# Seven block products in place of eight for the last matmul of an attention and feed-forward kernel

## The chip, the cores and the metric

The kernel runs on one core of a Trainium2 chip. The time is that of the device for one execution, in microseconds (us). Before the change it is 239.63 us, the median of three runs (239.34 to 240.02).

## The reference, cut to what matters

```python
q_s = softmax(q, axis=-1)                       # q, k, v: 8 batches, 8 heads, 576 tokens, 64 wide
k_s = softmax(k, axis=tokens)
kv = einsum('bhsd,bhse->bhde', k_s, v)
x = einsum('bhsd,bhde->bhse', q_s, kv)          # laid out as 4608 tokens x 512
a, b = x @ w1, x @ w2                           # 4608 x 1024 each
out = ((a * b) @ w3) @ w_out                    # 4608 x 512
```

## The kernel before

Both last weights are folded once: `W3O = w3 @ w_out` (1024 x 512) is made by `fold`, so that the feed-forward part is `(a * b) @ W3O`. Inputs are float32; the operands of TensorE are float16.

The work has two halves. `attention(b)`, for the batches 0 to 7, makes the 512 main tokens of its batch (`x`, as float16) and the 64 that remain of it (`xtail`). `chunk(c)`, for c = 0 to 7, takes the main tokens of batch c, and chunk 8 all the tails. The steps of a batch are: row maximum of q (`qmx`, L582), subtraction (`qsub`, L587), exponential on ScalarE (`qexp`, L595), sum (`qsm`, L600), a small number added (`qeps`, L606 or L608), reciprocal (`qrc`, L612), product (`qn`, L619) and a transpose by DMA (`qd`), each in two parts; for k a maximum (`kmx`, L489 or L498 to L501, then `cba`, `cbx`, `cb`), a subtraction (`ksub`, L524) and an exponential (`kexp`, L532); v is cast (`vc`). `kv` (L549) multiplies k and v, `kve` and `kv2` (L566 to L575) scale the result, `xm` and `xt` (L667) apply it to the transposed q, and `xs`, `xts` copy the products to `x` and `xtail`.

A chunk has eight pairs of `up` steps (L784), of four matmuls each with 512 moving columns (in the chunks 0 and 1, which are cut in two halves of tokens, eight with 256). The pair's first product goes to SBUF by `bs`, on ScalarE or VectorE; VectorE then multiplies it with the second, which it reads from PSUM (`ab`, L799). Four `down` steps follow, one for each 128 tokens (L806, for chunk 8 L821): eight matmuls with 512 moving columns over `ab` and `W3O`. `os` copies their bank to SBUF, and `st` stores it with two DMAs.

A list of 795 names, `ORDER`, sets what stands before what on each engine, and `PICKS` which engine takes a step that could run on several. Each engine works through its own part of the list in order and waits at each step for what that needs. Rings of buffers add waits: four PSUM banks for `up` (`pab`), two for `down` (`po`), two for attention, two `ab` tiles; so `ab` of chunk c overwrites that of chunk c - 2. Steps marked as `port` have two inputs in SBUF, or are GpSimd's (`qsub`, `ksub`, `qn`, the `kmx` of batches 0 to 3, some casts). Where two of them that follow each other in the list are on different engines, `run` makes the second wait for the first. It does so for the list's first 580 entries (`LINKED`), up to about `xm` of batch 6.

Of the kernel before, what the change touches and what calls it, by code (L numbers as in the profile page):

```python
# [101 lines left out]
up.1.2.0.3 up.0.2.0.3 down.1.2 kexp.3.1 kv.3 qmx.4.1 bs.2.0.3 os.1.1 qn.3.1 qd.3.1 qn.3.0 vc.4.1
qsub.4.1 qmx.4.0 ab.2.0.2 kmx.4.0 kve.3 up.1.2.0.4 up.0.2.0.4 os.1.2 kv2.3 bs.2.0.4 up.1.2.0.5 xt.2
bs.2.0.5 xts.2.1 qexp.4.1 down.1.3 ab.2.0.3 up.0.2.0.5 xts.2.0 ab.2.0.4 os.1.3 qd.3.0 xm.3.0 xm.3.1
xt.3 qmx.5.0 cba.4 ab.2.0.5 xs.3.0.0 cbx.4 xts.3.1 up.1.2.0.6 up.0.2.0.6 xts.3.0 xs.3.1.0 xs.3.0.1
cb.4 qsub.4.0 qsub.5.0 vc.4.0 xs.3.1.1 bs.2.0.6 st.1.0 qsm.4.1 ab.2.0.6 up.1.2.0.7 up.0.2.0.7
up.1.3.0.0 up.0.3.0.0 bs.2.0.7 qeps.4.1 qrc.4.1 ab.2.0.7 down.2.0 st.1.2 up.1.3.0.1 up.0.3.0.1 k.5
down.2.1 qexp.4.0 qsm.4.0 qeps.4.0 qexp.5.0 ksub.4.1 bs.3.0.0 kexp.4.1 ksub.4.0 kexp.4.0 qrc.4.0
st.1.1 v.5 qn.4.0 bs.3.0.1 os.2.0 st.1.3 qd.4.0 up.1.3.0.2 kv.4 kve.4 os.2.1 down.2.2 qn.4.1 kmx.5.1
kmx.5.0 cba.5 qmx.5.1 kv2.4 down.2.3 cbx.5 bs.3.0.2 qd.4.1 ab.3.0.0 up.0.3.0.2 ab.3.0.1 xm.4.0  # L110
os.2.2 os.2.3 xm.4.1 cb.5 ab.3.0.2 xt.4 xts.4.0 xs.4.0.0 up.1.3.0.3 xts.4.1 up.0.3.0.3 qsm.5.0
up.1.3.0.4 xs.4.1.0 qsub.5.1 qexp.5.1 bs.3.0.3 qeps.5.0 up.0.3.0.4 up.1.3.0.5 ab.3.0.3 q.6 bs.3.0.4
st.2.0 k.6 ksub.5.0 xs.4.1.1 ab.3.0.4 up.0.3.0.5 up.1.3.0.6 bs.3.0.5 qsm.5.1 qrc.5.0 up.0.3.0.6
ab.3.0.5 up.1.3.0.7 up.0.3.0.7 ksub.5.1 qn.5.0 xs.4.0.1 kexp.5.0 vc.5.0 bs.3.0.6 qeps.5.1 kexp.5.1
vc.5.1 ab.3.0.6 up.1.4.0.0 up.0.4.0.0 qrc.5.1 bs.3.0.7 qmx.6.1 ab.3.0.7 kv.5 down.3.0 down.3.1
st.2.1 qd.5.0 st.2.2 bs.4.0.0 kmx.6.0 kmx.6.1 os.3.0 up.1.4.0.1 down.3.2 os.3.1 qmx.6.0 kve.5 kv2.5
ab.4.0.0 qn.5.1 qd.5.1 up.0.4.0.1 xm.5.0 qsub.6.1 bs.4.0.1 qexp.6.1 os.3.2 xm.5.1 xt.5 xs.5.1.0
cba.6 ab.4.0.1 up.1.4.0.2 up.0.4.0.2 xts.5.0 xts.5.1 up.1.4.0.3 up.0.4.0.3 qsub.6.0 bs.4.0.2 qsm.6.1
ab.4.0.2 qexp.6.0 cbx.6 bs.4.0.3 xs.5.1.1 xs.5.0.1 qeps.6.1 cb.6 xs.5.0.0 ksub.6.0 v.7 q.7 ab.4.0.3
qrc.6.1 up.1.4.0.4 bs.4.0.4 up.0.4.0.4 up.1.4.0.5 bs.4.0.5 ab.4.0.4 up.0.4.0.5 ab.4.0.5 up.1.4.0.6  # L120
bs.4.0.6 qmx.7.0 up.0.4.0.6 up.1.4.0.7 up.0.4.0.7 ab.4.0.6 up.1.5.0.0 up.0.5.0.0 bs.4.0.7 down.3.3
up.1.5.0.1 qsm.6.0 st.3.1 ksub.6.1 kexp.6.1 kexp.6.0 qn.6.1 ab.4.0.7 st.3.0 v.6 vc.6.1 vc.6.0 kv.6
k.7 st.2.3 os.3.3 down.4.0 down.4.1 st.3.2 st.3.3 qd.6.1 qeps.6.0 bs.5.0.1 kve.6 os.4.0 os.4.1
kmx.7.0 kmx.7.1 qrc.6.0 qn.6.0 bs.5.0.0 ab.5.0.0 up.0.5.0.1 up.1.5.0.2 up.0.5.0.2 up.1.5.0.3
ab.5.0.1 kv2.6 qmx.7.1 bs.5.0.2 ab.5.0.2 qd.6.0 down.4.2 up.0.5.0.3 xm.6.0 bs.5.0.3 ab.5.0.3 cba.7
os.4.2 xm.6.1 xt.6 xts.6.0 xts.6.1 up.1.5.0.4 up.0.5.0.4 bs.5.0.4 up.1.5.0.5 ab.5.0.4 bs.5.0.5
xs.6.1.1 up.0.5.0.5 up.1.5.0.6 up.0.5.0.6 xs.6.0.1 cbx.7 xs.6.1.0 bs.5.0.6 ab.5.0.5 up.1.5.0.7
up.0.5.0.7 vc.7.0 xs.6.0.0 down.4.3 qsub.7.1 qsub.7.0 qexp.7.0 qexp.7.1 cb.7 ab.5.0.6 st.4.2 st.4.0
ksub.7.1 qsm.7.0 qeps.7.0 qrc.7.0 bs.5.0.7 ab.5.0.7 ksub.7.0 vc.7.1 up.1.6.0.0 up.0.6.0.0 up.1.6.0.1
up.0.6.0.1 st.4.1 qsm.7.1 kexp.7.1 bs.6.0.0 up.1.6.0.2 ab.6.0.0 up.0.6.0.2 kexp.7.0 kv.7 bs.6.0.1  # L130
qeps.7.1 ab.6.0.1 up.1.6.0.3 bs.6.0.2 up.0.6.0.3 up.1.6.0.4 qrc.7.1 ab.6.0.2 bs.6.0.3 ab.6.0.3
up.0.6.0.4 up.1.6.0.5 up.0.6.0.5 kve.7 bs.6.0.4 os.4.3 qn.7.1 qd.7.1 qn.7.0 qd.7.0 kv2.7 down.5.0
os.5.0 ab.6.0.4 down.5.1 os.5.1 bs.6.0.5 ab.6.0.5 down.5.2 up.1.6.0.6 os.5.2 bs.6.0.6 xm.7.0 xm.7.1
xt.7 xts.7.0 up.0.6.0.6 up.1.6.0.7 xs.7.0.1 xs.7.1.0 xs.7.0.0 xs.7.1.1 xts.7.1 up.0.6.0.7 up.1.7.0.0
bs.6.0.7 ab.6.0.6 up.0.7.0.0 up.1.7.0.1 bs.7.0.0 down.5.3 st.4.3 os.5.3 st.5.3 st.5.1 st.5.2
ab.6.0.7 ab.7.0.0 up.0.7.0.1 up.1.7.0.2 up.0.7.0.2 bs.7.0.1 up.1.7.0.3 ab.7.0.1 up.0.7.0.3 bs.7.0.2
up.1.7.0.4 ab.7.0.2 up.0.7.0.4 bs.7.0.3 up.1.7.0.5 ab.7.0.3 bs.7.0.4 ab.7.0.4 up.0.7.0.5 up.1.7.0.6
up.0.7.0.6 bs.7.0.5 ab.7.0.5 bs.7.0.6 up.1.7.0.7 ab.7.0.6 bs.7.0.7 up.0.7.0.7 ab.7.0.7 up.1.8.0.0
up.0.8.0.0 up.1.8.0.1 up.0.8.0.1 down.6.0 bs.8.0.0 bs.8.0.1 st.5.0 os.6.0 st.6.0 down.6.1 os.6.1
down.6.2 down.6.3 os.6.2 os.6.3 down.7.0 up.1.8.0.2 bs.8.0.2 down.7.1 st.6.1 st.6.2 ab.8.0.0  # L140
ab.8.0.1 st.6.3 os.7.0 os.7.1 down.7.2 up.0.8.0.2 up.1.8.0.3 ab.8.0.2 bs.8.0.3 up.0.8.0.3 up.1.8.0.4
up.0.8.0.4 ab.8.0.3 bs.8.0.4 ab.8.0.4 up.1.8.0.5 bs.8.0.5 up.0.8.0.5 up.1.8.0.6 bs.8.0.6 ab.8.0.5
up.0.8.0.6 ab.8.0.6 up.1.8.0.7 up.0.8.0.7 bs.8.0.7 ab.8.0.7 down.7.3 st.7.0 os.7.2 down.8.0 st.7.1
# [784 lines left out]
```

## Time and profile before

| What | Number |
|---|---|
| Median of three runs | 239.63 us |
| Span of the profiled execution, first to last instruction | 237.4 us |
| What the runs' median holds beside that span | 2.2 us |
| TensorE's granted clock, whole span | 1.00 |
| Busy in the span: TensorE | 230.1 us (97%) |
| VectorE | 180.3 us (76%) |
| ScalarE | 121.7 us (51%) |
| GpSimd | 110.0 us (46%) |

An execution's own time outside the profiler is not listed beside its span, so that the 2.2 us stand for what lies around it. The profile names engines PE (TensorE), PEld (its loading of weights), DVE (VectorE), ACT (ScalarE), POOL (GpSimd) and SP (the queue that issues DMAs). In a row of grouped instructions come the line, the engine, the operation, output and inputs with their shapes, the count, the busy time, the mean duration of one, and the idle time ahead of them. Consecutive instructions of one engine overlap a little, so the distance from start to start is shorter than a duration. Row by row in time, a row gives its start, its length (of several instructions where x2 or more stands at the end) and in brackets how long the engine was idle before it and what released it.

### The profile page before, as it was taken

Reading aid. Unit: us, or ns where it says so; the run is one execution under the profiler, and the core shown is the slowest. Engines: PE = TensorE matmul, PEld = TensorE weight load, DVE = VectorE, ACT = ScalarE, POOL = GpSimd, SP = SyncE. Lnnn points to the kernel's source line nnn. Section 1 sums busy time; section 2 is a strip of 40 time slices with the busy share of each in tenths; the row PEclk is TensorE's granted clock in tenths of the full one; section 3 lists DMA queues with packets and bytes.
Section 4 is the critical chain, followed back from the end, with each engine's and each line's share of the span. In section 5 each row is a group of like instructions: output and inputs, shape, how many; then the busy total and the mean of one; then the engine's idle time right before and its main releaser. Section 6 shows DMA issues by size and latency. Waiting matters only on the chain.

```text
span 237.4 us, 4860 instructions
## 1 busy us (share of the span) xinstructions
PE 230.1 (97%) x1935; PEld 119.5 (50%) x1935; DVE 180.3 (76%) x277; ACT 121.7 (51%) x221; POOL 110.0 (46%) x73
## 2 busy tenths in 40 slices
...
DMA packets 38742, 46.51 MB, mean 196 GB/s; under 512 B 17088, under 2 KB 22976, under 8 KB 38720
## 3 DMA queue, kind: packets, MB, share of 16 engines
...
q14 instruction: 7, 0.06, 0.1%
...
## 4 chain that ended last, share of the span: by engine, by line
PE 81%; DMA 8%; DVE 5%; POOL 4%; issue 1%; ACT 0%; POOLq 0%; ACTq 0%
PE pab L784 46%; PE po L806 22%; DMA w<-in_moe_w_dram 6%; PE po L457 4%; PE po L821 3%; PE pkv L549 2%; DMA qT<-en 2%; PE xm L667 1%; DVE qm L582 1%; POOL k L524 1%; PE w3t L445 1%; POOL en L619 1%; POOL w L406 1%; DVE ab L799 1%; DVE kmx L498 1%
## 5 line engine op out<-in xcount | busy, mean ns | idle before, releaser
L784 PE MATMUL pab<-x,w1sb 128*128 128x512 f16 (+1 forms) x320 | 65.9, 337 | 0.4 <-DVE kmx L499 0.4
L784 PE MATMUL pab<-x,w2sb 128*128 128x512 f16 (+1 forms) x320 | 66.0, 337 | 0.0
L799 DVE TENSOR_TENSOR ab<-pab,bsb 128x512 f16<-128x512 f32 x72 | 48.6, 682 | 20.2 <-PE pab L784 13.6
L806 PE MATMUL po<-W3O,ab 128*128 128x512 f16 x256 | 58.9, 379 | 0.0
L784 PEld LDWEIGHTS <-w1sb 128*128 128x128 f16 x352 | 34.2, 98 | 28.5 <-DMA w1sb<-in_moe_w_dram 0.6
L784 PEld LDWEIGHTS <-w2sb 128*128 128x128 f16 x352 | 33.5, 98 | 27.5 <-issue 0.7
L325 ACT CAST bsb<-pab 128x512 f16<-128x512 f32 x46 | 26.8, 582 | 35.8 <-PE pab L784 34.6
L524 POOL TENSOR_TENSOR k<-k,cb 128x1152 f32<-128x1152 f32 x12 | 31.4, 2628 | 16.4 <-issue 5.1
L806 PEld LDWEIGHTS <-ab 128*128 128x128 f16 x256 | 24.5, 98 | 28.5 <-issue 0.4
L587 POOL TENSOR_TENSOR q<-q,qm 128x1024 f32<-128x1024 f32 (+1 forms) x14 | 29.5, 2125 | 13.1 <-DVE rc L573 5.4
L325 ACT COPY osb<-po 128x512 f32<-128x512 f32 (+1 forms) x25 | 14.3, 571 | 40.3 <-PE po L806 26.8
L619 POOL TENSOR_TENSOR en<-eq,qr 128x1024 f16<-128x1024 f16 (+1 forms) x13 | 27.2, 2106 | 10.5 <-DVE qr L612 10.4
L582 DVE TENSOR_REDUCE qm<-q 128x20 f32<-128x1280 f32 (+1 forms) x16 | 21.2, 1340 | 3.6 <-DMA q<-in_q_dram 3.6
L325 DVE CAST bsb<-pab 128x512 f16<-128x512 f32 x26 | 17.6, 677 | 6.8 <-PE pab L784 6.3
L600 DVE TENSOR_REDUCE qr<-eq 128x20 f32<-128x1280 f16 (+1 forms) x16 | 21.5, 1341 | 1.5 <-ACT eq L595 1.4
L595 ACT ACTIVATE eq<-q 128x1280 f16<-128x1280 f32 (+1 forms) x16 | 18.5, 1161 | 4.8 <-DVE q L587 3.9
L532 ACT ACTIVATE ek<-k 128x1152 f16<-128x1152 f32 x16 | 18.2, 1163 | 3.8 <-POOL k L524 3.8
L489 DVE TENSOR_REDUCE km<-k 128x128 f32<-128x1152 f32 x8 | 16.9, 2149 | 0.0
L457 PE MATMUL po<-wosb,w3T 128*128 128x512 f16 x64 | 15.3, 379 | 0.5 <-DMA wosb<-in_moe_w_out_dram 0.5
L325 DVE COPY osb<-po 128x512 f32<-128x512 f32 x12 | 8.3, 688 | 9.1 <-PE po L806 7.9
L329 ACT ACTIVATE x<-xm 128x512 f16<-128x512 f32 x18 | 10.3, 597 | 6.4 <-PE xm L667 6.2
L325 ACT CAST v<-v 128x1152 f16<-128x1152 f32 x9 | 10.3, 1148 | 0.3 <-DMA v<-in_v_dram 0.3
...
## 6 DMA issues: line engine op xcount, KB each, us to landing
...
k<-in_k_dram SPq DMA_DIRECT2D x4, 1152.0 KB, 10.1
...
```

Source lines behind the costliest of these rows:

```text
L325: return [(nc.scalar.copy if eng == "ACT" else engine[eng].tensor_copy)(out=out, in_=in_)]
L457: nc.tensor.matmul(st["pf", ft], lhsT=st["w3T", ft][:, gt, :], rhs=wosb[:, gt, :], start=(gt == 0), stop=(gt == N_FT - 1))
L524: return [engine[eng].tensor_tensor(out=kb[:, two(hp), :, :], in0=kb[:, two(hp), :, :], in1=st["cb", b][:, two(hp), None, :].broadcast_to( ...
L532: nc.scalar.activation(out=st["ek", b][:, hp, :, :].rearrange("p j (i d) -> p i j d", i=2), in_=kb[:, two(hp), :, :], func=AF.Exp)
L582: dve.tensor_reduce(out=st["qm", b][:, :, j], in_=qb[:, :, j, :], axis=AX.X, op=ALU.max)
L587: return [engine[eng].tensor_tensor(out=qb[:, :, j, :], in0=qb[:, :, j, :], in1=st["qm", b][:, :, j, None].broadcast_to([P, HH, n, D]), op ...
L595: nc.scalar.activation(out=st["eq", b, p], in_=qb[:, :, j, :], func=AF.Exp)
L600: dve.tensor_reduce(out=st["qr", b][:, :, slice(*PARTS[p])], in_=st["eq", b, p], axis=AX.X, op=ALU.add)
L619: return [engine[eng].tensor_tensor(out=st["en", b][:, j, :, :].rearrange("p j h d -> p h j d"), in0=st["eq", b, p], in1=st["qr", b][:, :, ...
L784: nc.tensor.matmul(st["p", one, c, sub, u][:, a * (t1 - t0):(a + 1) * (t1 - t0)], lhsT=w[:, ct, fb * P:(fb + 1) * P], rhs=x()[:, ct, t0:t1 ...
L799: dve.tensor_tensor(out=st["ab", c][:, nf * u:nf * u + nf, t0:t1], in0=cut(st["p", 0, c, sub, u]), in1=cut(st["bsb", c, sub, u]), op=ALU.mult)
L806: nc.tensor.matmul(st["po", c, tb], lhsT=st["ab", c][:, ft, tb * P:(tb + 1) * P], rhs=W3O[:, ft, :], start=(ft == 0), stop=(ft == N_FT - 1))
```

## The change

For the chunks 2 to 7 (`SEVEN`), the four `down` steps become seven products of blocks. `ab` is cut into 2 x 2 blocks of 512 features by 256 tokens, `W3O` into 2 x 2 blocks of 512 features by 256 columns. Each product (`sp`) is two times four matmuls with 256 moving columns. The blocks that they need are sums:

- `sT.1` to `sT.4`, once for the whole kernel: four sums of blocks of `W3O`, 128 x 1024 in float16, two on VectorE and two on GpSimd. They are written to the tile of w3, which nothing reads after the fold.
- `sa.c.1` to `sa.c.4` for each chunk: four sums of blocks of `ab`, of the same size and type; 12 of the 24 on VectorE and 12 on GpSimd.

The results are put together in three PSUM banks, taken in turn from the ring of two. The products 1, 6, 5 and 3 add up in one; after each of the first three a copy of the bank's state goes to SBUF as float32 (`kept`, 128 x 512, 15 on ScalarE and 3 on VectorE), and the next product waits for that copy. Product 2 has a bank of its own, and 7 and then 4 share the third, where 4 waits until `os.c.22` has read it. Four blocks come out: 12 by a copy, and 11, 22 and 21 by VectorE, which adds a bank and a kept copy. Each is stored by two DMAs as before, with runs of 256 columns in place of 512.

`ab` of chunk c + 2 now waits for products and sums of chunk c. The ring of the kept copies (`w3T`) has three buffers instead of two. `LINKED` goes from 580 to 10000, so the chaining of `port` steps, the new sums among them, holds for the whole list. From the entry after `up.0.1.1.2` on (the 260th) the list is new, with 859 names, and so are the engines picked for it: `bs` has 53 steps on ScalarE where it had 46, `ksub` 13 on GpSimd where it had 12.

VectorE's queue, at the place where batch 4's row sums have been inverted and chunk 3 begins (L612 before, L622 after). Before (`ab_1318` is chunk 2's):

```order
L600 TENSOR_REDUCE qr_1596<-eq_1513 128x4x5
L799 TENSOR_TENSOR ab_1318<-pab_1576,bsb_1592 128x512
L612 RECIPROCAL qr_1596<-qr_1596 128x4x5
L799 TENSOR_TENSOR ab_1318<-pab_1604,bsb_1619 128x512
L600 TENSOR_REDUCE qr_1596<-eq_1655 128x4x4
L524 TENSOR_TENSOR k32_0_75<-k32_0_75,cb_1586 128x1152
L612 RECIPROCAL qr_1596<-qr_1596 128x4x4
```

Of the change (`ab_1328` is chunk 2's, `ab_1650` chunk 3's; `w316_90` is the tile that holds the sums):

```order
L622 RECIPROCAL qr_1548<-qr_1548 128x4x4
L622 RECIPROCAL qr_1548<-qr_1548 128x4x5
L811 TENSOR_TENSOR ab_1328<-pab_1599,bsb_1612 128x512
L592 TENSOR_REDUCE qm_1641<-q32_1_78 128x4x4
L811 TENSOR_TENSOR ab_1650<-pab_1620,bsb_1618 128x512
L592 TENSOR_REDUCE qm_1641<-q32_1_78 128x4x5
L811 TENSOR_TENSOR ab_1650<-pab_1636,bsb_1648 128x512
L983 TENSOR_TENSOR w316_90<-W3O_89,w316_90 128x1024
L854 TENSOR_TENSOR w316_90<-ab_1328 128x1024
L811 TENSOR_TENSOR ab_1650<-pab_1655,bsb_1745 128x512
L499 TENSOR_REDUCE km_1758<-k32_1_76 128x128
```

The `ksub` of batch 4 has left VectorE, and two sums stand between two `ab` steps; the first of them waits, by the chain, for GpSimd's `qn` of batch 4.

GpSimd's queue, from `qn` of batch 4 to `ksub` of batch 5. Before:

```order
L619 TENSOR_TENSOR en_1672<-eq_1655,qr_1596 128x4x4x64
L619 TENSOR_TENSOR en_1672<-eq_1513,qr_1596 128x4x5x64
L587 TENSOR_TENSOR q32_1_78<-q32_1_78,qm_1557 128x4x320
L524 TENSOR_TENSOR k32_1_76<-k32_1_76,cb_1830 128x1152 x2
L619 TENSOR_TENSOR en_1922<-eq_1659,qr_1857 128x4x4x64
```

Of the change:

```order
L629 TENSOR_TENSOR en_1610<-eq_1476,qr_1548 128x4x4x64
L629 TENSOR_TENSOR en_1610<-eq_1565,qr_1548 128x4x5x64
L983 TENSOR_TENSOR w316_90<-W3O_89 128x1024
L983 TENSOR_TENSOR w316_90<-W3O_89,w316_90 128x1024
L597 TENSOR_TENSOR q32_1_78<-q32_1_78,qm_1641 128x4x320
L854 TENSOR_TENSOR w316_90<-w316_90,ab_1328 128x1024
L854 TENSOR_TENSOR w316_90<-ab_1328 128x1024
L597 TENSOR_TENSOR q32_1_78<-q32_1_78,qm_1641 128x4x256
L597 TENSOR_TENSOR q32_0_77<-q32_0_77,qm_1830 128x4x256
L597 TENSOR_TENSOR q32_0_77<-q32_0_77,qm_1830 128x4x320
L534 TENSOR_TENSOR k32_1_76<-k32_1_76,cb_1920 128x1152 x2
```

Four sums and the `qsub` of batch 6 now stand ahead of the `ksub` of batch 5.

The diff, without the two tables:

```diff
-LINKED = 580
+LINKED = 10000
...
-    plan = Plan({"pab": 4, "po": 2, "att": 2, "osb": 4, "eq": 4, "bsb": 4, "w3T": 2}, PICKS, ORDER)
+    plan = Plan({"pab": 4, "po": 2, "att": 2, "osb": 4, "eq": 4, "bsb": 4, "w3T": 3}, PICKS, ORDER)
...
+    sums = [w316[:, x, :].rearrange("p (f t) -> p f t", f=4) for x in range(N_FT)]
+    SEVEN = [2, 3, 4, 5, 6, 7]
+    DONE = {}
+    BANK = {1: 0, 6: 0, 5: 0, 3: 0, 2: 1, 7: 2, 4: 2}
...
+        def sums_of(i, eng):
+            a = st["ab", c]
+            a11, a12, a21, a22 = [a[:, 4 * f:4 * f + 4, 256 * t:256 * t + 256]
+                                  for t in range(2) for f in range(2)]
+            in0, in1, op = {1: (a21, a22, ALU.add), 2: (sums[4], a11, ALU.subtract),
+                            3: (a11, a21, ALU.subtract), 4: (a12, sums[5], ALU.subtract)}[i]
+            return [engine[eng].tensor_tensor(out=sums[3 + i], in0=in0, in1=in1, op=op)]
+
+        def product(i):
...
+            for tb in range(2):
+                for ft in range(4):
+                    t, f0, t0 = left
+                    r, g0, c0 = right
+                    nc.tensor.matmul(
+                        st["ps", c, bank][:, tb * 256:tb * 256 + 256],
+                        lhsT=t[:, f0 + ft, t0 + tb * P:t0 + tb * P + P],
+                        rhs=r[:, g0 + ft, c0:c0 + 256],
+                        start=fresh and tb == 0 and ft == 0, stop=ft == 3, skip_group_check=True)
+
+        def kept(i, eng):
+            st["kept", c, i] = work.tile([P, 512], F32, tag="w3T", name="kept", bufs=3)
+            copy(eng, st["kept", c, i], st["ps", c, 0])
+
+        def block(n, eng):
...
+            i, bank = {11: (1, 1), 22: (3, 2), 21: (2, 2)}[n]
+            dve.tensor_tensor(out=st["osb", c, n], in0=st["ps", c, bank], in1=st["kept", c, i],
+                              op=ALU.add)
...
-              ([("down", c - 2, 3)] if c > 1 else ...
+              (DONE[c - 2] if c > 1 else ...
+        if c in SEVEN:
...
+            for i, needs in ((3, lo), (1, lo + hi), (2, [("sa", c, 1)]), (4, [("sa", c, 2)])):
+                A(("sa", c, i), {"POOL": (1.9, True), "DVE": (0.69, True)}, 0,
+                  lambda eng, i=i: sums_of(i, eng), needs + last)
+            for i, needs, taken in (
+                    (2, hi, 1), (1, lo, 1), (7, [("sa", c, 3)], 1),
+                    (6, [("sa", c, 2), ("kept", c, 1)], 0), (5, [("sa", c, 1), ("kept", c, 2)], 0),
+                    (3, [("sa", c, 4), ("kept", c, 3)], 0), (4, hi + [("os", c, 22)], 0)):
+                A(("sp", c, i), "PE", 0.87, lambda i=i: product(i),
+                  needs + folded + [("sT", x) for x in range(1, 5)], takes="po" if taken else None)
...
+            DONE[c] = [("sp", c, x) for x in (1, 2, 4)] + [("sa", c, x) for x in (3, 4)]
```

More of the change, by code (lines that the diff above doesn't have):

```diff
@@ L102 @@
[L102 to L143, printed above, removed]
@@ L144 @@
-st.7.2 os.7.3 os.8.0 down.8.1 down.8.2 st.7.3 os.8.1 os.8.2 st.8.0 down.8.3.0 os.8.3.0 down.8.3
-os.8.3 st.8.1 st.8.2 st.8.3.0 st.8.3
+ab.1.1.1 cb.3 up.1.1.1.2 up.0.1.1.2 st.0.2 v.3 bs.1.1.2 qsub.3.1 xm.2.1 qsub.3.0 up.1.1.1.3 ksub.3.1
+xs.2.1.1 q.4 os.1.0 ab.1.1.2 xs.2.1.0 kmx.4.0 up.0.1.1.3 bs.1.1.3 up.1.2.0.0 qexp.3.0 bs.2.0.0
+ab.1.1.3 qsm.3.0 up.0.2.0.0 qexp.3.1 qmx.4.0 vc.3.0 qeps.3.0 ksub.3.0 ab.2.0.0 vc.3.1 v.4 up.1.2.0.1
+qrc.3.0 up.0.2.0.1 down.1.2 qsub.4.0 up.1.2.0.2 qsm.3.1 os.1.1 kexp.3.0 kexp.3.1 up.0.2.0.2 qn.3.0
@@ new lines @@
+qeps.3.1 down.1.3 kmx.4.1 vc.4.1 bs.2.0.1 qrc.3.1 st.1.0 qmx.4.1 kv.3 up.1.2.0.3 bs.2.0.2 ab.2.0.1
+cba.4 ab.2.0.2 qexp.4.0 qn.3.1 kve.3 qsub.4.1 kv2.3 bs.2.0.3 os.1.2 cbx.4 st.0.3 up.0.2.0.3 q.5 cb.4
+qd.3.0 up.1.2.0.4 bs.2.0.4 os.1.3 ab.2.0.3 up.0.2.0.4 sT.1 up.1.2.0.5 xt.2 xts.2.0 xts.2.1
+up.0.2.0.5 ab.2.0.4 qsm.4.0 bs.2.0.5 up.1.2.0.6 ab.2.0.5 qd.3.1 xm.3.0 qexp.4.1 k.5 xs.3.0.1 xm.3.1
+ksub.4.1 ksub.4.0 qsm.4.1 xs.3.1.1 v.5 up.0.2.0.6 bs.2.0.6 st.1.2 ab.2.0.6 xs.3.0.0 up.1.2.0.7
+qeps.4.0 qrc.4.0 up.0.2.0.7 xs.3.1.0 up.1.3.0.0 qn.4.0 bs.2.0.7 qeps.4.1 qrc.4.1 qn.4.1 vc.4.0
@@ new lines @@
+bs.4.0.5 v.6 sp.3.7 qd.5.1 ab.4.0.4 sp.3.5 up.0.4.0.5 kept.3.3 os.3.22 up.1.4.0.6 st.2.21 cbx.6
+kve.5 ab.4.0.5 cb.6 sp.3.4 sp.3.3 vc.6.1 up.0.4.0.6 up.1.4.0.7 bs.4.0.6 qn.5.0 kv2.5 qsm.6.0 st.2.12
+os.3.12 qd.5.0 os.3.21 qexp.6.1 xm.5.1 xm.5.0 xt.4 ab.4.0.6 xs.5.1.0 xs.5.1.1 xs.5.0.0 vc.6.0
+up.0.4.0.7 bs.4.0.7 xts.4.1 sp.4.1 st.3.21 ab.4.0.7 xs.5.0.1 qsm.6.1 ksub.6.0 xts.4.0 up.1.5.0.0
+ksub.6.1 qeps.6.0 up.0.5.0.0 kexp.6.0 qrc.6.0 sa.4.1 bs.5.0.0 up.1.5.0.1 ab.5.0.0 kexp.6.1 bs.5.0.1
+up.0.5.0.1 up.1.5.0.2 sa.4.2 k.7 qmx.7.0 st.3.22 ab.5.0.1 kept.4.1 bs.5.0.2 up.0.5.0.2 sp.4.6
@@ new lines @@
+up.1.5.0.3 sa.4.4 kmx.7.0 qeps.6.1 bs.5.0.3 qrc.6.1 st.3.11 ab.5.0.2 up.0.5.0.3 kept.4.2 up.1.5.0.4
+kmx.7.1 st.3.12 sp.4.5 kv.6 bs.5.0.4 sa.4.3 xt.5 qn.6.0 vc.7.0 qsub.7.0 ab.5.0.3 sp.4.7 up.0.5.0.4
+kept.4.3 cba.7 qn.6.1 sp.4.3 os.4.22 up.1.5.0.5 xts.5.0 qmx.7.1 cbx.7 qd.6.0 kve.6 kv2.6 sp.4.4
+os.4.12 qexp.7.0 cb.7 xts.5.1 sp.4.2 os.4.21 os.4.11 bs.5.0.5 up.0.5.0.5 qd.6.1 ab.5.0.4 up.1.5.0.6
+st.4.21 ab.5.0.5 xm.6.1 xs.6.1.1 xm.6.0 xs.6.0.0 xs.6.1.0 xs.6.0.1 st.4.22 ksub.7.1 bs.5.0.6 sa.5.3
```

93 lines of the change are left out of this document (85 added, 8 removed), and 77 rows, old and new, of the table PICKS.

## The prediction, made before the result was known

> **What bounds the kernel now.** I read the page's busy shares first, then the chain of work that ended last in order of time, then a table of stages, then the groups of instructions by shape.
>
> ```profile
> span 237.4 us, 4860 instructions
> PE 230.1 (97%) x1935; PEld 119.5 (50%) x1935; DVE 180.3 (76%) x277; ACT 121.7 (51%) x221; POOL 110.0 (46%) x73
> 75.97 8.76 PE pab L784 x48
> 84.73 1.73 PE po L806 x8
> 227.41 6.95 PE po L821 x40
> 234.43 0.37 ACT osb L325
> ```
>
> TensorE is busy for 97% of the span, and from 75.97 us on the chain is TensorE without a break, down to the 6.95 us of chunk 8's last matmuls and the final copy and store. So a microsecond less of TensorE work after 75.97 is a microsecond less of time, if no other engine holds TensorE up. The 76% of VectorE is a mean over unlike stages; the change begins close to 75.97, and what the others have to spare there is read from the stage:
>
> ```profile
> 75.97:139.73 63.76, 63.76 (x554) 30.20 (x554) 59.94 (x89) 47.61 (x89) 46.83 (x22) 1.00 0.90 272
> 160.00:180.00 20.00, 20.00 (x163) 9.27 (x161) 13.61 (x24) 10.03 (x16) 8.18 (x4) 1.00 0.22 44
> 200.00:220.00 20.00, 20.00 (x95) 9.10 (x93) 8.92 (x14) 1.17 (x2) 0.00 (x0) 1.00 0.34 79
> ```
>
> After the stretch come the busy times of TensorE, of its weight loads, of VectorE, ScalarE and GpSimd, then the clock. In the first row, up to the end of chunk 4's `up` steps, VectorE is busy for 59.94 of 63.76 us: 3.82 us idle. Later it has 6 and 11 us idle in 20. What the change puts on VectorE decides in the first stage and hardly after it.
>
> **What TensorE gains.** The price of a matmul by its moving columns comes from the chain's pieces. Eight with 512 columns take 1.73 us, 0.216 each. For 256 columns I take a piece in which all 48 have that shape:
>
> ```profile
> 56.86 5.24 PE pab L784 x48
> L784 PE MATMUL pab<-x,w2sb 128*128 128x256 f16 x128 | 16.7, 273 | 0.0
> L806 PEld LDWEIGHTS <-ab 128*128 128x128 f16 x256 | 24.5, 98 | 28.5 <-issue 0.4
> ```
>
> That is 0.109 each. The group's row gives 0.130 (16.7 / 128), the other end, but its steps stand partly in stretches where TensorE waited. Each product needs its own weights for each matmul; a load takes 98 ns, 11 ns less than the matmul that hides it, as it was in the piece of 48. So a product is 8 x 0.109 = 0.87 us, seven are 6.11, four `down` steps were 6.92: **0.81 us less for a chunk, 4.84 for six.** (At 0.130 it would be 7.28, and 2.2 us more for six.) The span's beginning and its tail stay: the tail's 40 matmuls are the same. Before, `down.7.3` covered chunk 8's last `ab`; now the first seven matmuls of `down.8.0` (1.51 us) do, and `ab` takes 0.68. Against the profiled execution that is 237.4 - 4.84 = 232.6 us of span; with the 2.2 us around it, 239.63 - 4.84 = 234.8.
>
> **What VectorE pays in the first stage.** Durations:
>
> ```profile
> L799 DVE TENSOR_TENSOR ab<-pab,bsb 128x512 f16<-128x512 f32 x72 | 48.6, 682 | 20.2 <-PE pab L784 13.6 <-PE po L806 3.6 <-ACT bsb L325 2.1
> L325 DVE COPY w3T<-w3t 128x1024 f16<-128x1024 f16 x2 | 1.4, 685 | 0.2 <-PE w3t L445 0.2
> L619 DVE TENSOR_TENSOR en<-eq,qr 128x1024 f16<-128x1024 f16 x1 | 1.2, 1225 | 0.0
> L524 DVE TENSOR_TENSOR k<-k,cb 128x1152 f32<-128x1152 f32 x4 | 5.3, 1351 | 0.0
> 127.24 0.68 DVE L799 TENSOR_TENSOR ab<-pab,bsb 128x512 f16<-128x512 f32 x1
> 127.84 0.43 DVE L505 STREAM_TRANSPOSE kmq<-km 128x256 f32<-128x256 f32 x1
> ```
>
> An addition of a bank and a kept copy is an `ab` in all but its type: 0.68 us, and 0.60 from its start to the next one's (127.24 to 127.84). A sum of 1024 float16 elements with two float16 inputs is in no row. It is bounded by the copy of 1024 float16 elements, 0.685, and by the product whose second input is float32, 1.225. I take 0.685, since all its operands are float16 as the copy's are, and 0.60 from start to start. I counted the lists from `up.1.1.1.3` to `up.0.4.0.7`. TensorE has the same work there in both: nine `down` steps before, two `down` and 14 products now (12.1 us against 12.2). VectorE gains seven sums, six additions and one `ab` (14 x 0.60 = 8.4) and loses four `bs` (2.4), a `ksub` (1.35), a `qmx` (1.3), four `xts` (0.8), and a `qrc` and a `qeps` (0.3): **+2.25 us.** 59.94 + 2.25 = 62.2 of 63.8, so that 1.6 us of idle time are left where there were 3.82.
>
> The idle time's causes in that stage:
>
> ```profile
> DVE ab L799 <- PE pab L784: 1.1, 3, 0.4
> DVE mxe L518 <- ACT mx L514: 0.9, 2, 0.7
> DVE ab L799 <- ACT bsb L325: 0.5, 1, 0.5
> DVE xtail L331 <- PE xt L667: 0.3, 1, 0.3
> ```
>
> Of 3.82 us some 1.4 are waits for TensorE, which a later VectorE wouldn't have; the others stay. The chain adds waits for GpSimd in their place (next part). I take the idle time as unchanged, 3.8; then TensorE is held up by what was added, **2.25 us.** The ends are 0 (the idle time falls to 1.6) and what the slow rival says. `bs` in front of `ab`, and `kept` in front of a product, lie on ScalarE: it gains six copies and two casts net, some 5 us, 53 of 63.8, and between a product and the one that needs its copy the list puts other TensorE work of 0.9 to 1.7 us, more than a copy's:
>
> ```profile
> L325 ACT COPY osb<-po 128x512 f32<-128x512 f32 x23 | 13.5, 588 | 39.5 <-PE po L806 26.8 <-PE po L821 10.1 <-issue 2.6
> ```
>
> So I cost them at nothing; without that cover each of 18 would cost up to 0.6. The stores keep their bytes; their halved runs I cost at nothing too, as the DMA engines' share in the later rows above is 0.22 and 0.34.
>
> **What GpSimd and the chain pay.**
>
> ```profile
> L619 POOL TENSOR_TENSOR en<-eq,qr 128x1024 f16<-128x1024 f16 x7 | 13.4, 1908 | 9.1 <-DVE qr L612 9.1
> L587 POOL TENSOR_TENSOR q<-q,qm 128x1280 f32<-128x1280 f32 x7 | 16.3, 2340 | 9.6 <-DVE qm L582 3.9 <-issue 3.4 <-DVE rc L573 2.2
> POOL en L619 <- DVE qr L612: 6.1, 4, 2.8
> POOL q L587 <- DVE rc L573: 5.4, 2, 3.2
> POOL k L524 <- DMA out_dram<-osb: 4.7, 1, 4.7
> ```
>
> A sum of 1024 elements on GpSimd is taken at 1.91 us, which it needs whether its operands are float16 or float32. Five in the stage are 9.5: 46.8 + 9.5 = 56.4 of 63.8. The chain makes it stand still during VectorE's seven sums, 4.2 us, so 3.2 us are left of 16.9 idle. Those 16.9 were mostly waits for things that the order had come to too early (the last three rows); the new order puts a `qsub` or a sum there. On VectorE the chain puts GpSimd ahead of `sT.1`, `sT.2`, `sa.2.4` and `sa.3.1`. Behind each wait in VectorE's queue stands an `ab`, whose banks the `up` after next needs: a late GpSimd is a late TensorE.
>
> Whether a sum left unchained would be free is answered by three rows, the first two from beyond the 580 entries:
>
> ```profile
> 161.42 5.22 POOL L524 TENSOR_TENSOR k<-k,cb 128x1152 f32<-128x1152 f32 x2 [5.10 <-issue]
> 163.54 0.55 DVE L608 TENSOR_SCALAR qr<-qr 128x16 f32<-128x16 f32 x1
> L608 DVE TENSOR_SCALAR qr<-qr 128x20 f32<-128x20 f32 x2 | 0.3, 167 | 0.0
> ```
>
> VectorE's tiny L608, 167 ns elsewhere, took 0.55 us and ended at 164.09, as the first of GpSimd's two instructions did (161.42 + 5.22 / 2 = 164.03): unchained, an operation can be held behind GpSimd too, so I count the chain itself as no added price, only the order that it fixes.
>
> Do the two queues meet in time? I worked it out at `sa.3.1`, which GpSimd's second `ksub` of batch 5 must precede:
>
> ```profile
> 71.74 4.20 POOL L587 TENSOR_TENSOR q<-q,qm 128x1280 f32<-128x1280 f32 x2 [3.42 <-issue]
> L325 POOL CAST v<-v 128x1152 f16<-128x1152 f32 x5 | 5.7, 1146 | 0.0
> 86.46 0.71 PE pkv L549 x72
> 92.74 0.34 PE xm L667 x4
> 93.08 0.22 PE po L667 x4
> 93.30 0.06 PE pab L667 x8
> ```
>
> From 71.74 on GpSimd has eight `qsub` (17.0 us), six `ksub` (15.7), four `qn` (8.5), a cast (1.15) and four sums (7.6), and stands still for four sums of VectorE (2.4): 124.1 us at the earliest. TensorE has listed ahead of that place, from 75.97 on, 41 `up` (35.5), two `down` (3.5), nine products (7.8) and two batches' `kv`, `xm` and `xt` (2.7): 125.5. GpSimd has 1.4 us to lose in 50.
>
> **The rivals.**
>
> *Everything fits* (18%). VectorE's idle time drops to 1.6 us. For it: the list interleaves it finely. Against it: engines with 3% to spare. 239.63 - 4.84 = 234.8 us.
>
> *The chain slips* (slower, 27%). In the stage VectorE reaches four waits for GpSimd, whose instructions last about 2.2 us. If it arrives half an instruction early each time, that is 4.4 us of idle time more, 8.2 in all, and TensorE is held up by 8.2 - 1.6 = 6.6: 239.63 - 4.84 + 6.6 = 241.4. It decides from 6.4 us of idle VectorE in the stage on, where the loss equals 4.84. For it: only 3.2 of GpSimd's 16.9 idle us can stay. Against it: the sums at `sa.3.1` (124.1 against 125.5) let GpSimd come first. SBUF — State Buffer, section "SBUF: two separate sides", of the Trainium skill says that the pair of ports that these two engines share is locked for a whole instruction, by a VectorE operation with two SBUF inputs too; by that rule the rival would need no chain, since any sum that meets a GpSimd instruction waits. The row of L608 agrees for an operation with one input; no row here shows one with two.
>
> *The sums run at one element a cycle* (6%). Then seven sums in the stage cost 0.54 more each, 3.8 us: 237.0 + 3.8 = 240.8. VectorE: DVE Perf Modes, section "The perf-mode tier table", of the Trainium skill speaks against it: a two-input operation on 16-bit data in SBUF runs at two elements a cycle; its 1224 ns for 2048 would make about 0.69 for 1024 (an estimate from that page). No row here shows such an operation.
>
> **How the numbers follow.** The forecast (49%): 239.63 - 4.84 + 2.25 = **237.0 us**, with its own range from 235.5 to 238.9. The range that should hold the time 8 times in 10 is 234.8 (everything fits) to 241.4 (the slow rival's price). A measurement of this kernel tells about 0.3% from no change, 0.7 us: faster is below 238.9, slower above 240.35. Faster: the forecast's share less a small part that spills over, and the case that fits: 0.60. Between: 0.12, the forecast's spill and the mild end of the chain's slip. Slower: the rest of the slip and the slow sums, 0.28.
>
> **What would show each step.** The products' rows should show 336 matmuls with 256 columns at about 0.109 us of TensorE time each; 0.12 or more, or weight loads in the waits, would make the first term wrong. The sums on VectorE should read about 0.69 us, the additions 0.68. In a stage of the same work TensorE's idle time should be about 2 us, released by VectorE's `ab` or the sums, and VectorE's idle time near 3.8 us, with GpSimd among its releasers. If TensorE is idle for more than 4.8 us after 75.97, I am wrong about the sign; if it waits for `kept`, then about ScalarE.

## The result and the profile after

The changed kernel takes **235.37 us** (median of four runs, 234.93 to 235.70) against 239.63. The ratio is 0.982, with a 95% interval from 0.981 to 0.984: 4.26 us less. The profiled execution took 235.63 us.

The page's first lines and a part of its groups, of the changed kernel:

```profile
span 233.9 us, 5195 instructions
PE 224.9 (96%) x2079; PEld 133.2 (57%) x2079; DVE 186.6 (80%) x289; ACT 129.3 (55%) x240; POOL 143.0 (61%) x88
...
L854 POOL TENSOR_TENSOR w<-ab 128x1024 f16<-128x1024 f16 x6 | 12.7, 2124 | 14.8 <-DVE ab L811 14.7
...
L870 PE MATMUL po<-w 128*128 128x256 f16 x144 | 18.2, 273 | 0.0
...
L335 ACT COPY kept<-po 128x512 f32<-128x512 f32 x15 | 8.8, 587 | 12.9 <-PE po L870 12.9
```

TensorE is 5.2 us less busy, VectorE 6.3 and GpSimd 33 us more. The groups of VectorE, by shape, show what the new operations cost there:

```profile
L886 DVE TENSOR_TENSOR osb<-po,kept 128x512 f32<-128x512 f32 x18 | 12.1, 679 | 4.3 <-PE po L870 2.1 <-ACT kept L335 2.1
L854 DVE TENSOR_TENSOR w<-ab 128x1024 f16<-128x1024 f16 x6 | 4.1, 685 | 0.3 <-POOL k L534 0.2
L983 DVE TENSOR_TENSOR w<-W3O 128x1024 f16<-128x1024 f16 x1 | 0.7, 672 | 0.0
L983 DVE TENSOR_TENSOR w<-W3O,w 128x1024 f16<-128x1024 f16 x1 | 0.7, 681 | 0.0
```

A sum of 1024 float16 elements takes about 0.68 us on VectorE, and the same on GpSimd 2.12. The table of stages, with columns as before; the first row covers the same TensorE work as the 63.76 us from 75.97 to 139.73 of the kernel before, but for one `xt` of some 0.2 us that now falls behind it:

```profile
76.09:140.48 64.39, 64.09 (x602) 35.72 (x603) 61.32 (x90) 50.61 (x95) 57.72 (x28) 1.00 0.86 253
160.00:180.00 20.00, 20.00 (x198) 12.01 (x196) 13.51 (x24) 9.69 (x19) 14.46 (x7) 1.00 0.32 68
200.00:220.00 20.00, 20.00 (x133) 12.19 (x126) 11.16 (x19) 2.95 (x6) 6.33 (x3) 1.00 0.20 46
```

The crowded stage became 0.63 us longer, not 2.25: VectorE is 1.38 us busier in it, and its idle time went from 3.82 to 3.07. TensorE is idle for 0.30 us of it (64.39 - 64.09), where it was never idle before. The rest of TensorE's path, from the stage's end to the last matmul, went from 94.63 us (139.73 to 234.36) to 90.05 (140.48 to 230.53), 4.58 less. The two together are 3.95 us less. After 76 us TensorE's rows in time show one wait:

```profile
108.23 1.02 PE L796 MATMUL pab<-x,w1sb 128*128 128x512 f16 x4 [0.19 <-DVE ab L811]
109.09 1.04 PE L870 MATMUL po<-W3O,ab 128*128 128x256 f16 x8
109.97 1.03 PE L796 MATMUL pab<-x,w2sb 128*128 128x512 f16 x4
```

From 109.09 to 109.97 a product takes 0.88 us between two starts; in the chain of waits two of them stand together with 0.875 each:

```profile
155.22 1.75 PE po L870 x16
...
223.59 6.94 PE po L833 x40
```

So the gain looks like the eighth product, 4.26 of the 4.84 us that were counted for it. What had to be found out is whether it is that, and why VectorE, with 3.8 us to spare, took it so well.

### The profile page after: what moved, and what is told of

It is laid out like the page before. It is cut to its first block, busy times and chain, and to the rows that moved or that the text cites. A ratio compares the mean times of both kernels' runs of the same rounds, so it can differ in the third digit from the quotient of the medians.

```text
span 233.9 us, 5195 instructions
## 1 busy us (share of the span) xinstructions
PE 224.9 (96%) x2079; PEld 133.2 (57%) x2079; DVE 186.6 (80%) x289; ACT 129.3 (55%) x240; POOL 143.0 (61%) x88
## 4 chain that ended last, share of the span: by engine, by line
PE 72%; DMA 20%; DVE 4%; POOL 1%; issue 1%; ACT 1%; POOLq 0%; DVEq 0%
PE pab L796 45%; PE po L870 16%; DMA q<-in_q_dram 6%; DMA k<-in_k_dram 6%; DMA w1sb<-in_moe_w_dram 5%; PE po L818 5%; PE po L833 3%; DMA qT<-en 2%; PE pkv L559 2%; DVE ab L811 1%; PE xm L677 1%; DVE qm L592 1%; DVE km L499 1%; POOL w L416 1%; PE po L677 1%
## 5 line engine op out<-in xcount | busy, mean ns | idle before, releaser
L335 ACT CAST bsb<-pab 128x512 f16<-128x512 f32 x53 | 30.6, 589 | 38.7 <-PE pab L796 38.3
L796 PEld LDWEIGHTS <-w1sb 128*128 128x128 f16 x352 | 33.8, 98 | 24.7 <-issue 1.0
L534 POOL TENSOR_TENSOR k<-k,cb 128x1152 f32<-128x1152 f32 x13 | 34.0, 2627 | 9.5 <-DVE km L511 3.0
L629 POOL TENSOR_TENSOR en<-eq,qr 128x1024 f16<-128x1024 f16 (+1 forms) x14 | 29.5, 2122 | 3.7 <-ACT qr L616 2.2
L854 POOL TENSOR_TENSOR w<-ab 128x1024 f16<-128x1024 f16 x6 | 12.7, 2124 | 14.8 <-DVE ab L811 14.7
L870 PEld LDWEIGHTS <-w 128*128 128x128 f16 x192 | 18.6, 98 | 5.6
L854 POOL TENSOR_TENSOR w<-ab,w 128x1024 f16<-128x1024 f16 x5 | 10.6, 2122 | 13.1 <-DVE w L854 12.2
L870 PE MATMUL po<-w 128*128 128x256 f16 x144 | 18.2, 273 | 0.0
L870 PEld LDWEIGHTS <-ab 128*128 128x128 f16 x144 | 14.1, 98 | 5.1
L335 DVE CAST bsb<-pab 128x512 f16<-128x512 f32 x19 | 12.9, 679 | 4.7 <-PE pab L796 4.7
L335 ACT COPY kept<-po 128x512 f32<-128x512 f32 x15 | 8.8, 587 | 12.9 <-PE po L870 12.9
```

The costliest lines, as they stand in the source:

```text
L335: return [(nc.scalar.copy if eng == "ACT" else engine[eng].tensor_copy)(out=out, in_=in_)]
L534: return [engine[eng].tensor_tensor(out=kb[:, two(hp), :, :], in0=kb[:, two(hp), :, :], in1=st["cb", b][:, two(hp), None, :].broadcast_to( ...
L629: return [engine[eng].tensor_tensor(out=st["en", b][:, j, :, :].rearrange("p j h d -> p h j d"), in0=st["eq", b, p], in1=st["qr", b][:, :, ...
L796: nc.tensor.matmul(st["p", one, c, sub, u][:, a * (t1 - t0):(a + 1) * (t1 - t0)], lhsT=w[:, ct, fb * P:(fb + 1) * P], rhs=x()[:, ct, t0:t1 ...
L854: return [engine[eng].tensor_tensor(out=sums[3 + i], in0=in0, in1=in1, op=op)]
L870: nc.tensor.matmul(st["ps", c, bank][:, tb * 256:tb * 256 + 256], lhsT=t[:, f0 + ft, t0 + tb * P:t0 + tb * P + P], rhs=r[:, g0 + ft, c0:c0 ...
```

## The experiments

The letters in the expectations are theories. A: TensorE sets the time, and the others have a little room left. B: VectorE's queue sets a good part of it. C, formed after the first runs: TensorE and VectorE, with GpSimd chained to it, are about level in the new list, so that more on any of them costs time, and less on one alone brings little. D: VectorE still hides a gain. E comes with the last run. All times are medians; the kernel before took 239.4 to 239.5 us beside them, and "the changed kernel" is the 235.37 above.

### Eight products instead of seven

```diff
-            for tb in range(2):
+            for tb in [0, 1] * (2 if i == 2 else 1):
```

> Product 2 of each of the chunks 2 to 7 is computed twice into its bank, so that TensorE does eight block products a chunk instead of seven; all else is the changed kernel. Theory A (TensorE bounds the time from 76 us on, and the other engines have room): six products of 0.875 us come back in full, 235.4 + 5.25 = 240.6 us. Theory B (in the first stage, to the end of chunk 4's up steps, VectorE's queue sets the pace): the two products of that stage, 1.75 us, lie in TensorE's shadow of VectorE, and only four count: 238.9 us.

240.65 us (240.47 to 240.69; ratio 1.005, 1.004 to 1.007). Product 2's matmuls come twice in each of six chunks, 6 x 0.875 = 5.25 us of TensorE; the time rose by 5.28. With eight products and all the sums, additions and copies still there, the kernel is slower than before the change, as A has it: **the product that is saved is the whole gain**, the new list brings none by itself, and what TensorE gets to do is paid in full.

### Six products

```diff
-            for tb in range(2):
+            for tb in range(0 if i == 3 else 2):
```

> Product 3 of each of the chunks 2 to 7 is left out, so that block 12 lacks a term; the sums, copies and stores stay. TensorE has six products of 0.875 us less. Theory A: 235.4 - 5.25 = 230.1 us. Theory B: the stage up to chunk 4 keeps its length, because VectorE's 61.3 busy us and 3.1 idle ones set it, so that four products count: 231.9 us, and more if the later stages don't give theirs in full.

234.26 us (233.94 to 235.67; ratio 0.980, 0.977 to 0.983): 1.1 us less for 5.25 us of TensorE taken away. Neither number held. TensorE's rows with a wait, after 76 us:

```profile
138.65 0.41 PE L677 MATMUL po<-qT,kv 64*64 64x512 f16 x4 [1.89 <-DVE ab L811]
158.11 0.41 PE L677 MATMUL po<-qT,kv 64*64 64x512 f16 x4 [0.46 <-DVE bsb L335]
180.75 0.41 PE L677 MATMUL xm<-qT,kv 64*64 64x512 f16 x4 [1.05 <-DMA qT<-en]
215.79 1.05 PE L870 MATMUL po<-W3O,ab 128*128 128x256 f16 x8 [0.25 <-DVE osb L335]
```

That is 3.65 us of waits where there were 0.19: 5.25 - 3.46 = 1.8, and the profiled span indeed fell by 1.7 (to 232.2). The next 5 us of TensorE are not to be had in this list. This gave theory C.

### VectorE's sums made twice

```diff
-            return [engine[eng].tensor_tensor(out=sums[3 + i], in0=in0, in1=in1, op=op)]
+            return [engine[eng].tensor_tensor(out=sums[3 + i], in0=in0, in1=in1, op=op)
+                    for _ in range(2 if eng == "DVE" else 1)]
```

(and the same for `sT`.)

> Each of the 14 sums that VectorE makes is made twice in a row: 0.60 us more VectorE work each, 8.4 in all, seven of them (4.2 us) in the stage up to chunk 4. Theory A: VectorE's 3.1 idle us in the stage take most of it, the time rises by at most 1.5 us, to 235.4 - 236.9. Theory B: the idle time stays, the stage grows by all that is added, 4.2 us: 239.6 us.

243.81 us (243.44 to 244.07; ratio 1.019, 1.017 to 1.020). The 14 repeated sums are 14 x 0.60 = 8.4 us from start to start, and the time rose by 8.4. The longest of TensorE's waits:

```profile
108.30 0.60 PE L677 MATMUL po<-qT,kv 64*64 64x512 f16 x4 [0.98 <-DVE kv L585]
138.37 1.03 PE L871 MATMUL po<-w,ab 128*128 128x256 f16 x8 [0.94 <-DVE osb L887]
143.29 0.41 PE L677 MATMUL po<-qT,kv 64*64 64x512 f16 x4 [1.29 <-DVE osb L887]
174.56 1.05 PE L871 MATMUL po<-w 128*128 128x256 f16 x8 [0.75 <-DVE w L854]
193.95 1.05 PE L871 MATMUL po<-w 128*128 128x256 f16 x8 [0.97 <-DVE w L854]
```

All that VectorE gets on top is paid too, more than B's number. The first three rows are its queue in the crowded stage. That stage alone, here from 75.99 to 144.95 us, takes 68.96 us, 4.57 more than in the changed kernel for seven sums more (4.2); VectorE is busy for 66.09 us of it and idle for 2.87, where it was for 3.07. So the 3 us of idle time took nothing in: A falls, and for this stage B has it right. In this execution another 3.4 us came behind it, where B expected none. The last two rows lie there, where VectorE has room (3.8 us idle from 160 to 180): it isn't its load that counts there, but that a product waits for this very sum. A repeated sum thus adds to the load and to a wait at once, and that the total equals what was added is partly chance.

### VectorE's sums cut to a sixteenth

```diff
-            return [engine[eng].tensor_tensor(out=sums[3 + i], in0=in0, in1=in1, op=op)]
+            n = 16 if eng == "DVE" else 256
+            return [engine[eng].tensor_tensor(out=sums[3 + i][:, :, 0:n], in0=in0[:, :, 0:n],
+                                              in1=in1[:, :, 0:n], op=op)]
```

(and the same for `sT`; the rest of each sum is left out.)

> VectorE's 14 sums are cut to a sixteenth of their elements (16 of 256 columns of each block), the rest of each sum is left out: about 0.45 us less VectorE work each, 6.3 in all, 3.2 of it up to chunk 4; waits and chain stay. Theory C (TensorE and VectorE are balanced, so that what is added to either counts and what is taken from one alone doesn't): TensorE's few tenths of idle time go, 234.7 to 235.4 us. Theory D (VectorE's queue alone sets the time, as the full 8.4 us of the doubled sums and the 1.1 of the missing product would have it): 229 to 231 us.

235.30 us (235.21 to 235.56; ratio 0.983, 0.981 to 0.984), no change, as C has it; VectorE was 6.2 us less busy, and no wait of TensorE is left. D falls: taking the sums' work off VectorE alone brings nothing that is clear of the runs' scatter.

### Six products, with less work on VectorE, and on GpSimd too

The edits of the last and the last but two together; then also with GpSimd's sums cut.

> Both cuts at once: product 3 is left out in six chunks (TensorE 5.25 us less) and VectorE's sums are a sixteenth of their size (VectorE 6.3 us less). Theory C: the two together give much more than each alone, most of TensorE's 5.25: 230.5 to 232 us. Theory D: no more than VectorE's cut alone gives, the missing product adds nothing.

232.76 us (232.36 to 232.86; ratio 0.972, 0.970 to 0.974), 0.8 us above the end of C's range.

> Product 3 left out and all sums, GpSimd's too, cut to a sixteenth (the rest of each is left out). With VectorE's alone cut the time was 232.8, and TensorE waited for the transposed q of two batches, which come behind GpSimd. If GpSimd is the third engine of the balance, its cut (about 2 us each, 27 in all) frees the rest of the missing product: 235.4 - 5.25 = 230.2 us, to 231. If something else holds TensorE there (the DMA itself, ScalarE), it stays at 232 to 233.

232.43 us (231.92 to 232.72; ratio 0.971, 0.969 to 0.972). With TensorE and VectorE both relieved 2.6 us are gained, more than by each alone (1.1 and 0.1), but not the 5.25. GpSimd's sums add 0.3 us to that, no more than the runs scatter. TensorE's waits in the second of the two:

```profile
90.04 1.02 PE L796 MATMUL pab<-x,w1sb 128*128 128x512 f16 x4 [0.28 <-DVE ab L811]
137.65 0.41 PE L677 MATMUL po<-qT,kv 64*64 64x512 f16 x4 [0.83 <-ACT eq L605]
179.22 0.41 PE L677 MATMUL xm<-qT,kv 64*64 64x512 f16 x4 [1.06 <-DMA qT<-en]
214.27 1.05 PE L872 MATMUL po<-W3O,ab 128*128 128x256 f16 x8 [0.26 <-DVE osb L335]
```

These 2.4 us make up the 2.3 that were not gained (5.25 - 2.94). The second and the third row are 1.9 of them: with one product less TensorE comes to the attention of a batch before its q has passed through exponential, product and transpose. Which link of that row of steps is the late one was not tried.

### The chain taken away

```diff
-LINKED = 10000
+LINKED = 260
```

> The new list, with no chaining of port steps beyond the list's first 260 entries, which are those of the kernel before. If the ports shut the later engine out for an instruction anyway (as L608's 0.55 us suggested), the chain costs and gains nothing: 235.4 within 0.7 us. If the chain is what holds engines up, GpSimd loses its 6.5 us of waits for it in the stage and the time falls below 234.7. If unordered meetings cost more than ordered ones, single GpSimd or VectorE instructions grow by a microsecond or more and the time rises above 236.1.

243.81 us (241.75 to 245.37; ratio 1.018, 1.012 to 1.024). The list is the same, all of its new part is unchained, and **8.4 us are lost**, 6.4 to 10.0 by the single runs. The trace is that of the shortest of them. VectorE's groups by shape:

```profile
L854 DVE TENSOR_TENSOR w<-ab 128x1024 f16<-128x1024 f16 x6 | 8.2, 1370 | 0.0
L509 DVE TENSOR_TENSOR kmx<-kmx 128x512 f32<-128x512 f32 x4 | 4.8, 1196 | 0.1
...
L983 DVE TENSOR_TENSOR w<-W3O 128x1024 f16<-128x1024 f16 x1 | 2.8, 2754 | 0.0
L983 DVE TENSOR_TENSOR w<-W3O,w 128x1024 f16<-128x1024 f16 x1 | 2.6, 2603 | 0.0
```

The same sum takes 2.75 us instead of 0.67, and the mean of six 1.37 instead of 0.685, because two of the six take 2.83 and 2.65. What it meets is seen in the rows in time, first VectorE's:

```profile
93.05 0.65 DVE L811 TENSOR_TENSOR ab<-pab,bsb 128x512 f16<-128x512 f32 x1
93.63 2.75 DVE L983 TENSOR_TENSOR w<-W3O 128x1024 f16<-128x1024 f16 x1
96.31 0.68 DVE L811 TENSOR_TENSOR ab<-pab,bsb 128x512 f16<-128x512 f32 x1
```

and GpSimd's:

```profile
93.21 5.65 POOL L534 TENSOR_TENSOR k<-k,cb 128x1152 f32<-128x1152 f32 x2
```

GpSimd's first instruction takes 2.62 us, to 95.83, and its second 3.08. VectorE's sum begins 0.4 us after the start of the first and ends 0.55 us after its end: it is shut out until GpSimd's instruction is done, and the `ab` behind it stands in line. (GpSimd's second instruction, which begins while the sum is still running, is 0.46 us longer than the first.) Four of VectorE's 14 sums are as long as this, three of them in the crowded stage. With the chain a sum that must wait has VectorE idle for 0.2 us there instead:

```profile
118.17 0.69 DVE L854 TENSOR_TENSOR w<-ab,w 128x1024 f16<-128x1024 f16 x1 [0.23 <-POOL q L597]
126.48 0.69 DVE L854 TENSOR_TENSOR w<-ab 128x1024 f16<-128x1024 f16 x1 [0.22 <-POOL k L534]
```

Over the span VectorE is busy for 197.7 us without the chain and for 186.6 with it. Not all of this is the sums': the `kmx` at 70.02 us, a step of the attention, takes 2.71 us instead of 0.69 beside GpSimd's `qsub`, and at 76.82, ahead of the crowded stage, TensorE waits 2.12 us for the `ab` behind it. That is a third of the 6.1 us by which this execution's span is the longer. SBUF — State Buffer, section "SBUF: two separate sides", of the Trainium skill says that the two engines share a port pair that is locked for a whole instruction; the sum at 93.63 agrees, with 2.75 us against 0.67.

### The chain cut where it ended before

```diff
-LINKED = 10000
+LINKED = 580
```

> Only the number LINKED is taken back, from 10000 to the old 580: the new list is chained up to the sums of chunk 4 and no further, so that seven of VectorE's 14 sums stay chained and seven don't. Theory C (the chain is worth what it is because VectorE has no time left in the stage up to about 140 us, where an instruction shut out behind GpSimd holds TensorE up; later VectorE has 6 to 9 us idle in 20): the time stays within 0.7 us of the changed kernel, 235.1 to 236.1 us. Theory E (each unchained meeting costs the same wherever it is): half of the 8.4 us that the whole chain was worth in the new list, so about 239.5 us, no gain left.

235.42 us (235.07 to 236.26; ratio 0.984, 0.982 to 0.986), the time of the changed kernel, as C has it. Eight of VectorE's 14 sums stay chained, one more than expected, and of the six others only one meets GpSimd: at 158.82 us it takes 2.63 us instead of 0.68. The group's row shows it:

```profile
L854 DVE TENSOR_TENSOR w<-ab 128x1024 f16<-128x1024 f16 x6 | 6.1, 1011 | 0.3 <-POOL k L534 0.2
```

That is 2.0 us more, and yet no wait of TensorE stands in its rows. E's number falls, and a sum that was shut out where VectorE had room cost no time; but that rests on one meeting. So the edit of `LINKED` itself did nothing; the chain that counts, over the list's entries 260 to 580, had been there at the old number.

### The chain alone, in the kernel before

```diff
-LINKED = 580
+LINKED = 10000
```

> The kernel before with nothing but the chain over its whole list (LINKED 10000). Beyond its first 580 entries VectorE has two port steps, of which one waited 0.39 us behind GpSimd, at a time when VectorE is idle for a third: 239.5 within 0.7 us if the chain matters only where VectorE has no room; 238 or less if the chain by itself is part of what the change gained.

239.61 us (ten runs, 239.27 to 239.94; ratio 1.001, 1.000 to 1.002): nothing.

### GpSimd's sums made twice, and none on GpSimd

The same repetition as above with `"POOL"`; then the 14 sums that `PICKS` gave to GpSimd set to VectorE (`"sT_3": "DVE"` and so on).

> GpSimd makes each of its 14 sums twice: 2.12 us more each, 29.7 in all, 10.6 of it (five sums) up to chunk 4, where it has 6.7 idle us. If GpSimd has that room, the stage grows by 10.6 - 6.7 = 3.9 us and the late sums cost little: 239 to 241 us. If the chain passes every delay on to VectorE and so to TensorE, as the doubled VectorE sums did (8.4 for 8.4), it costs most of 29.7: above 255 us.

260.06 us (258.84 to 260.81; ratio 1.087, 1.084 to 1.090): of 29.7 us more on GpSimd 24.7 arrive at the end. In the profiled execution TensorE waits for 18 us after 76, and its own instructions take 5.5 us more (230.4 busy, against 224.9) at a granted clock of 0.98. From the list of waits:

```profile
PEld L871 <- POOL w L854: 13.7, 4, 5.9
...
PE po L871 <- POOL w L854: 12.0, 4, 5.4
```

> All 28 sums on VectorE: GpSimd loses 14 x 2.12 = 29.7 us, VectorE gains 14 x 0.60 = 8.4, five of them (3.0 us) up to chunk 4. If VectorE's queue is what counts, as for the doubled sums, the time rises by at least the 3.0 us of the stage, 238.4 to 243.8 us. If GpSimd and its chain were the tighter of the two, the time stays or falls: at most 235.4 us.

243.34 us (241.76 to 245.06; ratio 1.017, 1.012 to 1.022). VectorE does 14 sums more, 8.4 us, and 8.0 are paid; the profiled execution, the shortest of the four, has 6.1 of them. So GpSimd's share of the sums is needed in this list, whose places were chosen for it. TensorE's waits:

```profile
115.64 1.05 PE L870 MATMUL po<-w 128*128 128x256 f16 x8 [2.19 <-ACT eq L605]
155.09 1.05 PE L870 MATMUL po<-w 128*128 128x256 f16 x8 [1.42 <-DVE w L854]
164.70 0.41 PE L677 MATMUL po<-qT,kv 64*64 64x512 f16 x4 [2.49 <-DVE w L854]
```

In two of the three rows the late thing is a sum. The first names ScalarE's exponential; whether a kept copy stood behind it in ScalarE's queue, or a sum was late, isn't settled.

### Four steps again in chunks 2 and 3

```diff
-    SEVEN = [2, 3, 4, 5, 6, 7]
+    SEVEN = [4, 5, 6, 7]
```

(with the list's and the picks' steps for these two chunks put back as `down`, `os` and `st`.)

> Chunks 2 and 3 go back to four down steps each, set where the products 2, 6, 5 and 3 stood in the list; their sums, copies and additions go (VectorE loses five sums and six additions in the first stage, 6.6 us; GpSimd three sums, 6.4 us), and ScalarE takes their eight copies. Theory C: TensorE has 2 x 0.81 = 1.6 us more and VectorE is no bound in the stage: 235.4 + 1.6 - 0.5 = 236.5 us. Theory D: VectorE's 6.6 us are gained: at most 233 us.

236.59 us (236.14 to 236.77; ratio 0.988, 0.986 to 0.990). The two chunks that lie in the crowded stage are worth 1.22 us, 0.61 each, and the four behind it (239.63 - 236.59) / 4 = 0.76 each, or 0.70 against the 239.40 of the kernel before beside it, of 0.81 that TensorE saves. So the trade pays even where VectorE is full, as C has it; that it pays less there isn't clear of the runs' scatter. None of the kernels that do the whole computation is better than the changed one.

## Why the prediction was right, and by how much it was off

The time lies inside the range, on the side that was forecast, 1.7 us below the forecast and 0.6 above the case in which everything fits. It is just below the forecast's own range, which began at 235.5, so that what came is nearer to the case that was given 18% than to the one that was given 49%; the range holds it because its lower end is that case. Step by step:

**What TensorE gains: right.** 0.87 us a product was predicted, 0.875 are seen, and the eighth product put back costs 5.28 us for 5.25. The weight loads' 98 ns stayed hidden.

**What VectorE pays: the step that failed.** "I take the idle time as unchanged, 3.8; then TensorE is held up by what was added, 2.25 us." The stage grew by 0.63, and TensorE, which was to be idle for about 2 us in it, is idle for 0.30, of which 0.19 is the one wait for VectorE's `ab`. (In the run with `LINKED` at 580, whose list is the same up to behind this stage, it takes 64.09 us, so that the 0.63 is good to some 0.3.) The durations were right (sums at 0.685 predicted, 0.67 to 0.69 measured; additions at 0.68 and 0.679), so the slow sums, at 1.22, are out. Of the 1.62 us between, 0.87 is work: VectorE's busy time rose by 1.38. The one `ab` more that I had counted (0.60) is not in the stage: its groups hold 25 in both kernels, so that VectorE ends the stage one `ab` further behind TensorE, and the work falls where it has room. The remaining 0.27 of my count was not taken apart. The other 0.75 is idle time that vanished, which I had named as the lower end and not believed:

```profile
DVE osb L886 <- ACT kept L335: 0.9, 1, 0.9
DVE ab L811 <- ACT bsb L335: 0.6, 1, 0.6
...
DVE x L341 <- PE po L677: 0.4, 1, 0.4
DVE w L854 <- POOL q L597: 0.2, 1, 0.2
DVE w L854 <- POOL k L534: 0.2, 1, 0.2
```

These are VectorE's waits in the changed kernel's stage. Of the 1.4 us for TensorE's `up` and `xt` nothing is left but 0.4 us for an attention product; the chain's waits for GpSimd, which I feared in their place, are 0.4 us in all. VectorE's room is used up almost exactly, but hardly overdrawn: with its sums cut to a sixteenth the time stays, and with the sums doubled the stage grows by 4.57 us for 4.2 more. For that second step the rule of the prediction, idle time that stays and a TensorE held up by what is added, is right; it was wrong for the first, in which waits for TensorE were there to be used up. That the list also takes some 6 us off VectorE in the stage (the `bs`, `ksub`, `qmx` and others of the prediction's count) belongs to it; no run puts these steps back.

**GpSimd and the chain: the meeting right, the price of the chain wrong.** I had GpSimd at `sa.3.1` at 124.1 us at the earliest and TensorE there at 125.5. GpSimd's rows before that place:

```profile
118.94 2.34 POOL L597 TENSOR_TENSOR q<-q,qm 128x1280 f32<-128x1280 f32 x1 [0.81 <-DVE w L854]
121.23 5.21 POOL L534 TENSOR_TENSOR k<-k,cb 128x1152 f32<-128x1152 f32 x2
```

It ended at 126.44, and VectorE waited 0.22 us for it, and the product ahead of that place in TensorE's list (`sp.3.1`) ran until 126.62. The meeting was a near thing, as counted; a part of the slip is the price of a sum, 2.12 us on GpSimd where I had 1.91, 0.21 too little for each. "I count the chain itself as no added price, only the order that it fixes" was half true: its new length costs nothing and brings nothing (235.42 with 580, 239.61 in the kernel before), but without it from the list's 260th entry on the change would lose, at 243.81. The row of L608 showed the price, and I didn't carry it to seven sums.

**The chain slips (27%):** it didn't. Its mechanism is real: a sum that meets GpSimd out of order is shut out for some 2 us (2.60 to 2.83 where it takes 0.68), and the time then even passes the rival's 241.4. The chain brings the two together within 0.2 us in the crowded stage.

**Copies and stores: right at nothing.** `kept` takes 0.587 us on ScalarE, and VectorE waits once in the stage, 0.9 us, for one, and 2.1 us in the whole span; no wait of TensorE for it is seen. The stores land after 2.5 us (median) where they took 2.6.

**The sum.** Between forecast and result lie 1.67 us (237.04 - 235.37). The stage gives 1.62 of them. The rest is small and has both signs: TensorE's path behind the stage gained 4.58 where 4.84 was counted (0.26 the other way, some 0.2 of it the `xt` that now lies there), the span's beginning and end are 0.12 and 0.33 longer, what lies around the profiled span is 0.5 shorter (235.63 - 233.9 = 1.7, against 2.2), and the median is 0.26 below the profiled execution. These were not looked into, and that they come to 0.05 together is luck.
